# Weight conversion at every second group, four tiles of v ahead of u, and the order of one attention group's work

## The chip, the cores and the metric

The kernel runs on one core of a Trainium2 chip. The metric is the device time of one execution in microseconds (us). The core has TensorE for matmuls (PE in the profile, PEld for its weight loads), VectorE (DVE), ScalarE (ACT), GpSimd (POOL) and SyncE (SP), which issues the DMAs here. Each engine works through its own queue in program order, and semaphores hold an instruction until what it reads is there.

## The reference, cut to what matters

Three blocks follow one another: banded attention, a gated MLP that mixes tokens, and a second mixer. The change touches the first, and the first products of the second.

```python
# attention: 2 batches, 8 heads, 768 positions, 64 per head
keep = is_sink | in_window          # first 4 positions, or the last 128
a = softmax(where(keep, q @ k.T / 8, -1e9))
x = (a @ v) -> [2, 768, 512]
# gated MLP
h = relu(x @ w_in);  u, v = h[..., :512], h[..., 512:]
v_n = layer_norm(v)
gated = u * (w_spatial @ v_n + b_spatial);  x2 = gated @ w_out
# mixer: w_tok1, w_tok2 over tokens, w_ch1, w_ch2 over channels -> out
```

The weights come as 64-bit floats. A float32 product is made of three products of a high and a low half (`mm3`, lines 55 to 60).

## The kernel before, in words

**Attention** is 24 groups `g`: 12 blocks `j` of 128 rows (6 for each batch), each in two phases of four heads (`ph` 0 and 1). `banded` (lines 339 to 399) is a software pipeline, written out by hand: iteration `n` holds a piece of several groups. In the order of the program these are the reciprocal row sums of group n+1 (`sums`, line 195, DVE), the transposes of the weights of group n (`a_transpose`, line 267, PE) and their copies out of PSUM (`a_out`, ACT line 275 and DVE line 278, tiles aT and aL), the scaling of group n+1 (`norm`, lines 246 to 250, POOL and ACT), the scores of group n+3 (`qk` on PE, line 188, `scores` on DVE, lines 213 to 218), the exponentials of group n+2 (`expo`, ACT, line 234); then `v_step` (POOL, line 285) and `sink_parts` (ACT and POOL, lines 257 to 259) on even n, `split_vs` at n = 1 and 13 (ACT line 156, DVE line 158), `step` (the next piece of a pending layer norm, lines 547 to 551), `pump` at n = -1 to 6 and a last `flush` at n = 7; then weights times values of group n-1 (`pv`, line 301, PE), and on even n the sink products (`sinks_mm`, line 320) and `x_out` (ACT line 329, DVE line 330), which writes the high and the low half of x^T (tiles xTH, xTL); last `sinks` on odd n, and `fill`.

**The conversion of w_in** is what `pump` does: one chunk of 128 rows by 512 columns takes three bit operations on DVE (lines 481, 485, 488); its high half is copied by ACT (line 499) and its low half subtracted by POOL (line 500) in the `flush` that the next `pump` calls. Four chunks belong to v (`w_v`) and four to u (`w_u`). `prefetch` keeps two chunks' loads ahead on SP's queue (line 462).

**The filler**: `fill` (line 433) gives PE products of x with w_in, up to a budget of 1900 per iteration, as soon as the needed block of x is there (`xdone`, one iteration after `x_out`). A v tile is four steps of cost 680 and ends in a Relu on ACT and a layer norm; a u tile is four steps of cost 520 and ends in a Relu. `start_x` (lines 418 to 424) lists them: for each batch and half three v tiles, then four u tiles. `fill_until` (line 441) forces a tile before `x_out` overwrites the block that it reads. What is left goes to `mlp` (lines 671 to 674) ahead of the gate products.

**PSUM**: the v and u tiles and the transposed sink weights share two buffers (tag fl); weights times values have one (tag pv), free again after both halves of `x_out`; the transposes have one (tag tr), free after aT and aL.

Of the kernel before, what the change touches and what calls it, by code (L numbers as in the profile page):

```python
# [8 lines left out]
F32R = mybir.dt.float32r  # L9
I32 = mybir.dt.int32  # L10
U32 = mybir.dt.uint32
AF = mybir.ActivationFunctionType
ALU = mybir.AluOpType
PSUM = bass.MemoryType.PSUM

P = 128
B, H, S, D = 2, 8, 768, 64
NB = S // P
DM = H * D
# [5 lines left out]
SK = 8  # L25
SR = 3 * 4 * SK
# [3 lines left out]
NG = B * NB * 2  # L30

LQ, LE, LN = 3, 2, 1
PUMPS = range(-1, 7)
BUDGET = 1900


def f32(ap):
    return ap.bitcast(F32)


class Kernel:
# [106 lines left out]
            nc.sync.dma_start(out=raw[0:SR], in_=self.vs[b])  # L148
            self.vsraw = raw

    def split_vs(self, b):

        nc = self.nc
        raw = self.vsraw
        t = self.vsb[b] = self.ap.tile([P, DM], F32R, name="vs", tag="vs", bufs=1)
        nc.scalar.activation(out=t[0:SR], in_=raw[0:SR], func=AF.Copy)
        r = slice(4 * SK, 8 * SK)
        nc.vector.tensor_tensor(out=t[r], in0=raw[r], in1=f32(t[r]), op=ALU.subtract)

    def slots(self, j):  # L160

# [177 lines left out]
    def banded(self):  # L339
        self.q, self.vb, self.vsb, self.ps_s, self.ss, self.e, self.sm, self.rs = {}, {}, {}, {}, {}, {}, {}, {}  # L340
        self.aT, self.ps_x, self.aS, self.dv, self.eS = {}, {}, {}, {}, {}
        NJ = B * NB
        self.kr = self.ap.tile([P, NC4, RING, KW], F32, name="kr")
        self.vf = self.ap, "vf", 2
        self.scalar_loads(self.cp)
        self.load_qk(0, 2)
        self.warm(10)
        self.load_qk(1)
        self.prefetch()
        self.load_v(0)  # L350
        self.load_qk(2)
        self.masks(self.ap)
        for n in range(-LQ, NG + 2):
            j, ph = divmod(n, 2)
            self.xdone = self.xnext
            if ph and n >= -1:
                if (n + 7) // 2 < NJ:
                    self.load_qk((n + 7) // 2)
                if (n + 3) // 2 < NJ:
                    self.load_v((n + 3) // 2)  # L360
            if 0 <= n + LN < NG:
                self.sums(n + LN)
            if 0 <= n < NG:
                self.a_transpose(n)
                self.a_out(n)
            if 0 <= n + LN < NG:
                self.norm(n + LN)
            if n + LQ < NG:
                self.qk(n + LQ)
                if n < 0:  # L370
                    self.warm(3)
                self.scores(n + LQ)
            if 0 <= n + LE < NG:
                self.expo(n + LE)
            if 0 <= n < NG and ph == 0 and j % NB:
                self.v_step(j)
                self.sink_parts(j)
            if n in (1, 13):
                self.split_vs(n // 12)
            self.step()  # L380
            if n in PUMPS:
                self.pump()
            if n == max(PUMPS) + 1:
                self.flush()
            if 0 <= n - 1 < NG:
                self.pv(n - 1)
                if ph == 0:
                    if (j - 1) % NB:
                        self.sinks_mm(j - 1)

                    self.fill_until(j - 1)
                    self.x_out(j - 1)
            if 0 <= n < NG and ph == 1 and j % NB:
                self.sinks(j)
            if n == NG - 4:
                self.raws = [self.spatial_load(r) for r in range(2)]
            self.fill(BUDGET)
        self.xdone = self.xnext
        self.vf = self.sp, "tmp", 4


    def start_x(self):

        self.xT = self.pair(("XH", "XL"), [P, NC4, S], "xT")
        self.w_v = self.pair(("WA", "WB"), [P, NC4, 512], "wv")
        self.w_u = self.pair(("UC", "UD"), [P, NC4, 512], "wu")
        self.wq, self.wstarted, self.wdone, self.half = [], 0, 0, None
        for c in range(NC4):
            self.queue_weight(self.w_in, slice(c * P, c * P + P), (512, 1024), tuple(x[:, c] for x in self.w_v))
        for c in range(NC4):  # L410
            self.queue_weight(self.w_in, slice(c * P, c * P + P), (0, 512), tuple(x[:, c] for x in self.w_u))
        self.vn = [self.pair((f"{x}H", f"{x}L"), [P, NB, 512], "vn") for x in "VN"]
        self.uT = [self.unit(f"U{b}", [P, NC4, S], F32, "uT") for b in range(B)]
        self.xdone = self.xnext = -1
        self.raws = []
        self.later = []

        self.fills = []
        for b in range(B):
            for half in range(2):  # L420
                for t in range(3 * half, 3 * half + 3):
                    self.fills.append((b * NB + t, b * NB + t, self.v_tile(b, t)))
                for d in range(NC4):
                    self.fills.append((b * NB + 3 * half + 2, b * NB + 3 * half, self.u_tile(b, d, half)))
# [238 lines left out]
    def mlp(self):  # L663
# [57 lines left out]
        slabs = [self.pair(x, [P, 4, DM], "c2") for x in (("WA", "WB"),)]  # L721
        self.w_ch2 = {}

        def queue_ch2(f):
            self.w_ch2[f] = tuple(x[:, f % 4] for x in slabs[f // 4])
            self.queue_weight(self.w_c2, slice(f * P, f * P + P), (0, DM), self.w_ch2[f])

        slabs = [self.pair(x, [P, 4, DM], "c2") for x in (("WA", "WB"),)]
        self.w_ch2 = {}

        def queue_ch2(f):
            self.w_ch2[f] = tuple(x[:, f % 4] for x in slabs[f // 4])
            self.queue_weight(self.w_c2, slice(f * P, f * P + P), (0, DM), self.w_ch2[f])

        slabs = [self.pair(x, [P, 4, DM], "c2") for x in (("WA", "WB"),)]
        self.w_ch2 = {}

        def queue_ch2(*fs):
            for f in fs:
                self.w_ch2[f] = tuple(x[:, f % 4] for x in slabs[f // 4])  # L740
# [1 line left out]

        queue_ch1(0, (2, 3))
        queue_ch2(0, 1, 2)
        queue_ch1(1, (2, 3))
        queue_ch2(3)
        for b in range(B):
            for j in range(2):
                self.tok1_tile(b, j)
                pump()  # L750
        slabs += [self.pair(x, [P, 4, DM], "c2") for x in (("UC", "UD"), ("VH", "VL"))]
        queue_ch2(4, 5)
        queue_ch1(2, (2, 3))
        queue_ch2(*range(6, NF))
# [13 lines left out]
        for n in range(NCH * NF + 1):  # L768
            if n < NCH * NF:
                ch, f = divmod(n, NF)  # L770
# [172 lines left out]
```

## Time and profile before

| what | value |
|---|---|
| median of 3 runs | 496.29 us (495.05 to 496.36) |
| the profiled execution | 494.53 us |
| its span, first to last instruction | 492.7 us |
| mean granted TensorE clock | 0.984 |
| busy: PE, DVE, ACT, POOL | 468.9, 279.7, 178.8, 146.7 us |
| attention and the filler | from the start to about 164 us |

A row of the timeline reads: start in us, duration in us, engine, line, operation, the tile written and the tiles read, and shapes; in brackets the idle time of the engine just before and what ended it. A row of the windows reads: the stretch, its length, then for each engine busy us and, in parentheses, its instructions; then the granted TensorE clock as a share of full speed, the DMA engines' share, and GB/s.

### The profile page before, as it was taken

How to read it: one execution, taken by the hardware profiler on the slowest of the kernel's cores; microseconds unless marked ns; L12 is line 12 of the kernel's file. 1: busy time of each engine (PE TensorE's matmuls, PEld its weight loads, DVE VectorE, ACT ScalarE, POOL GpSimd, SP SyncE). 2: the span in 40 equal slices, each digit the busy share in tenths (PEclk: the TensorE clock that was granted, in tenths of full speed). 3: DMA queues.
4: the chain of work that ended last, by engine and by line, in shares of the span. 5: the costliest groups of instructions: out<-in, count | busy, mean ns of one | idle time of the engine just before them, and what ended most of it. 6: DMA issues, size and time to landing. Idle time of an engine off the chain costs nothing.

```text
span 492.7 us, 6952 instructions
## 1 busy us (share of the span) xinstructions
PE 468.9 (95%) x2562; PEld 391.6 (79%) x2562; DVE 279.7 (57%) x633; ACT 178.8 (36%) x483; POOL 146.7 (30%) x164
## 2 busy tenths in 40 slices
PE   8579899999999999999999899999999999999994
PEld 7357687788898999988888578888888888888883
DVE  6899855866546399837989797666312211311112
ACT  4566876887655222335532222221002100010000
POOL 1356751363544566733443132223000000000000
PEclk9879899999999999999999999999999999999999
DMA  8745142202023032305544144220010000200002
GB/s 260 244 151 175 46 143 68 67 23 87 0 85 130 1 108 69 103 0 151 151 147 130 43 137 122 90 95 26 34 53 1 0 1 0 86 1 0 1 0 92
DMA packets 19722, 38.48 MB, mean 78 GB/s; under 512 B 1824, under 2 KB 8224, under 8 KB 19680
## 3 DMA queue, kind: packets, MB, share of 16 engines
q1 hardware_dynamic: 19248, 37.69, 24.1%
q8 instruction: 22, 0.36, 0.3%
q10 hardware_dynamic: 432, 0.26, 0.2%
q14 instruction: 20, 0.16, 0.1%
HBM read 34.80 MB, written 3.15 MB: 77 GB/s over the span
## 4 chain that ended last, share of the span: by engine, by line
PE 77%; DVE 14%; ACT 5%; issue 2%; POOL 1%; POOLq 0%; ACTq 0%
PE pso L60 7%; PE pso L58 7%; PE pso L59 7%; PE psc L60 6%; PE psc L58 6%; PE psc L59 6%; PE psg L58 3%; PE psg L60 3%; PE psg L59 3%; PE pv L301 3%; DVE wi L485 2%; PE ps L60 2%; PE ps L59 2%; PE ps L58 2%; ACT e L234 2%; PE psu L58 2%
## 5 line engine op out<-in xcount | busy, mean ns | idle before, releaser
L647 DVE SCALAR_TENSOR_TENSOR hh<-psc,hh 128x512 fp32r<-128x512 f32 x36 | 24.9, 691 | 128.0 <-ACT hh L646 127.9
L646 ACT ACTIVATE hh<-psc 128x512 fp32r<-128x512 f32 x36 | 21.5, 597 | 157.2 <-PE psc L60 157.2
L60 PE MATMUL pso<-c2H,hh 128*128 128x512 f32 x144 | 56.3, 391 | 1.1 <-DVE hh L647 1.1
L58 PE MATMUL pso<-c2H,hh 128*128 128x512 f32 x144 | 56.9, 395 | 0.0
L59 PE MATMUL pso<-c2L,hh 128*128 128x512 f32 x144 | 56.0, 389 | 0.0
L488 DVE SCALAR_TENSOR_TENSOR wi<-rawi,wi 128x512 int32<-128x512 int32 (+2 forms) x46 | 40.3, 876 | 1.6
L234 ACT ACTIVATE e<-s,nm 128x136 f32<-128x136 f32 (+1 forms) x96 | 37.6, 393 | 3.9 <-DVE nm L218 3.9
L485 DVE SCALAR_TENSOR_TENSOR wi<-rawi,wi 128x512 int32<-128x512 int32 (+2 forms) x46 | 36.4, 790 | 1.6
L481 DVE TENSOR_SCALAR wi<-rawi 128x512 int32<-128x512 int32 (+2 forms) x46 | 32.5, 707 | 1.4 <-POOL c1L L500 1.2
L60 PEld LDWEIGHTS pso<-c2H,hh 128*128 128x128 f32 x144 | 27.0, 188 | 7.3 <-DVE hh L647 1.6
L59 PE MATMUL psg<-wsTL,vnH 128*128 128x384 f32 x96 | 32.1, 334 | 0.0
L58 PE MATMUL psg<-wsTH,vnH 128*128 128x384 f32 x96 | 32.1, 334 | 0.0
L60 PE MATMUL psg<-wsTH,vnL 128*128 128x384 f32 x96 | 32.1, 334 | 0.0
L59 PEld LDWEIGHTS pso<-c2L,hh 128*128 128x128 f32 x144 | 27.1, 188 | 5.5
L58 PEld LDWEIGHTS pso<-c2H,hh 128*128 128x128 f32 x144 | 27.0, 188 | 5.3
L188 PE MATMUL sc<-kr,q 64*128 64x264 f32 (+2 forms) x192 | 28.7, 417 | 0.4 <-DVE nm L218 0.2
L60 PE MATMUL psc<-u2H,c 128*128 128x512 f32 x72 | 28.0, 389 | 0.0
L58 PE MATMUL psc<-u2H,c1H 128*128 128x512 f32 x72 | 28.0, 389 | 0.0
L60 PE MATMUL psc<-u2H,c1L 128*128 128x512 f32 x72 | 28.0, 389 | 0.0
L58 PE MATMUL psc<-u2H,c 128*128 128x512 f32 x72 | 28.0, 389 | 0.0
L59 PE MATMUL psc<-u2L,c 128*128 128x512 f32 x72 | 28.0, 389 | 0.0
L59 PE MATMUL psc<-u2L,c1H 128*128 128x512 f32 x72 | 28.0, 389 | 0.0
(143 smaller groups left out, 1106.6 us busy)
## 6 DMA issues: line engine op xcount, KB each, us to landing
rawi<-in_moe_w_ch SPq DMA_DIRECT2D x24, 512.0 KB, 3.5
rawi<-in_moe_w_in SPq DMA_DIRECT2D x8, 512.0 KB, 5.0
v<-in_v SPq DMA_DIRECT2D x12, 256.0 KB, 3.7
out_x<-o SPq DMA_DIRECT2D x12, 256.0 KB, 2.4
kr<-in_k SPq DMA_DIRECT2D x11, 272.0 KB, 4.7
q<-in_q SPq DMA_DIRECT2D x11, 256.0 KB, 4.6
raws<-in_w_spT SPq DMA_DIRECT2D x6, 384.0 KB, 4.1
rawi<-in_moe_w_out SPq DMA_DIRECT2D x4, 512.0 KB, 5.7
```

Of the source, the lines that this page charges most:

```text
L58: self.nc.tensor.matmul(ps, lh, rh, start=(first and i == 0), stop=False)
L59: self.nc.tensor.matmul(ps, lh, rl, start=False, stop=False)
L60: self.nc.tensor.matmul(ps, ll, rh, start=False, stop=(last and i == n - 1))
L188: nc.tensor.matmul(o, q[r, p, :], k, start=True, stop=True)
L234: nc.scalar.activation(out=self.e[j][:, 4 * ph + c, :u], in_=s[:, c, :u], func=AF.Exp, bias=nm[:, c : c + 1], scale=-1.0, accum_out=sm[:, ...
L301: nc.tensor.matmul(ps[h * D : (h + 1) * D, p, :], w[:, (2 * p + h) * D : (2 * p + h + 1) * D], self.aT[g][c][:, 2 * x + h, :], start=(p == ...
L481: V.tensor_scalar(out=wi, in0=hi, scalar1=3, scalar2=0x3FFFFFFF, op0=ALU.logical_shift_left, op1=ALU.bitwise_and,)
L485: V.scalar_tensor_tensor(out=wi, in0=hi, scalar=-0x40000000, in1=wi, op0=ALU.bitwise_and, op1=ALU.bitwise_or)
L488: V.scalar_tensor_tensor(out=wi, in0=lo, scalar=29, in1=wi, op0=ALU.logical_shift_right, op1=ALU.bitwise_or)
L646: nc.scalar.activation(out=h, in_=ps, func=AF.Relu)
L647: nc.vector.scalar_tensor_tensor(out=l, in0=ps, scalar=0.0, in1=f32(h), op0=ALU.max, op1=ALU.subtract)
```

## The change

The pumps run at n = -1, 0, 1, 2, 3, 5, 7, 9, and the last flush at n = 10. `split_vs` is cut in two: ACT's part at n = 2 and 14, DVE's part at n = 3 and 15. `pv`, `sinks_mm`, `fill_until` and `x_out` stand ahead of `v_step`, `sink_parts`, `split_vs`, `step` and the pump. The filler's list has four v tiles, four u tiles, two v tiles, four u tiles for each batch. In `mlp` two repeated definitions of the same slabs and of `queue_ch2` are gone; a third one, which stood after them, stays.

```diff
-PUMPS = range(-1, 7)
+PUMPS = (-1, 0, 1, 2, 3, 5, 7, 9)
@@ split_vs
-    def split_vs(self, b):
+    def split_vs(self, b, part):
-        t = self.vsb[b] = self.ap.tile([P, DM], F32R, name="vs", tag="vs", bufs=1)
-        nc.scalar.activation(out=t[0:SR], in_=raw[0:SR], func=AF.Copy)
-        r = slice(4 * SK, 8 * SK)
-        nc.vector.tensor_tensor(out=t[r], in0=raw[r], in1=f32(t[r]), op=ALU.subtract)
+        if part == 0:
+            t = self.vsb[b] = self.ap.tile([P, DM], F32R, name="vs", tag="vs", bufs=1)
+            nc.scalar.activation(out=t[0:SR], in_=raw[0:SR], func=AF.Copy)
+        else:
+            t = self.vsb[b]
+            r = slice(4 * SK, 8 * SK)
+            nc.vector.tensor_tensor(out=t[r], in0=raw[r], in1=f32(t[r]), op=ALU.subtract)
@@ banded
                 self.expo(n + LE)
+            if 0 <= n - 1 < NG:
+                self.pv(n - 1)
+                if ph == 0:
+                    if (j - 1) % NB:
+                        self.sinks_mm(j - 1)
+
+                    self.fill_until(j - 1)
+                    self.x_out(j - 1)
             if 0 <= n < NG and ph == 0 and j % NB:
                 self.v_step(j)
                 self.sink_parts(j)
-            if n in (1, 13):
-                self.split_vs(n // 12)
+            if n in (2, 3, 14, 15):
+                self.split_vs(n // 12, n % 2)
             self.step()
             if n in PUMPS:
                 self.pump()
             if n == max(PUMPS) + 1:
                 self.flush()
-            if 0 <= n - 1 < NG:
-                self.pv(n - 1)
-                if ph == 0:
-                    if (j - 1) % NB:
-                        self.sinks_mm(j - 1)
-
-                    self.fill_until(j - 1)
-                    self.x_out(j - 1)
@@ start_x
-                for t in range(3 * half, 3 * half + 3):
+                for t in range((0, 4)[half], (4, 6)[half]):
```

## Rows read from the trace of the kernel before

**Rows 1.** Busy time in stretches of the span (columns as told above)

```profile
28.00:33.30 5.30, 4.25 (x27) 2.89 (x24) 5.13 (x16) 3.64 (x14) 3.38 (x4) 0.50 0.87 282
...
54.00:57.50 3.50, 3.50 (x17) 2.59 (x14) 3.40 (x13) 2.15 (x10) 2.42 (x4) 0.51 0.01 2
...
66.00:72.00 6.00, 5.43 (x48) 4.62 (x48) 2.80 (x18) 4.00 (x18) 1.88 (x2) 1.00 0.08 25
90.00:142.00 52.00, 51.84 (x413) 42.58 (x413) 34.31 (x126) 37.40 (x125) 25.61 (x42) 1.00 0.14 42
142.00:164.00 22.00, 21.82 (x115) 20.06 (x114) 10.95 (x13) 10.00 (x17) 11.85 (x12) 1.00 0.34 120
```

**Rows 2.** PE's waits for x^T's low half, whole run: total us, times, the longest

```profile
PE pv L301 <- DVE xTL L330: 3.4, 4, 1.6
```

**Rows 3.** Timeline of DVE, iterations n = 0 to 2, and its wait at n = 8

```profile
17.48 1.23 DVE L195 TENSOR_SCALAR r<-sums 128x4 f32<-128x4 f32 x1
...
21.84 0.68 DVE L158 TENSOR_TENSOR vs<-vsraw,vs 32x512 fp32r<-32x512 f32 x1 [1.13 <-ACT vs L156]
22.55 1.42 DVE L481 TENSOR_SCALAR wi<-rawi 128x512 int32<-128x512 int32 x1
...
25.34 0.16 DVE L195 TENSOR_SCALAR r<-sums 128x4 f32<-128x4 f32 x1
...
28.01 0.42 DVE L481 TENSOR_SCALAR wi<-rawi 128x512 int32<-128x512 int32 x1
...
29.81 0.68 DVE L330 TENSOR_TENSOR xTL<-pv,xTH 128x512 fp32r<-128x512 f32 x1
...
62.77 0.69 DVE L330 TENSOR_TENSOR xTL<-pv,xTH 128x512 fp32r<-128x512 f32 x1 [0.81 <-ACT xTH L329]
```

**Rows 4.** Timeline of POOL and ACT: two low halves, and one high half of a chunk

```profile
16.94 1.74 POOL L500 TENSOR_TENSOR wvL<-wi,wvH 128x512 fp32r<-128x512 f32 x1 [2.20 <-ACT wvH L499]
22.40 1.29 POOL L500 TENSOR_TENSOR wvL<-wi,wvH 128x512 fp32r<-128x512 f32 x1 [2.77 <-ACT wvH L499]
57.53 0.61 ACT L499 ACTIVATE wuH<-wi 128x512 fp32r<-128x512 f32 x1
```

**Rows 5.** Timeline of PE, iterations n = 3, 5 and 7

```profile
26.44 0.87 PE L267 MATMUL tr<-ident,e 128*128 128x128 f32 x4 [2.86 <-DVE aL L278]
...
30.55 0.69 PE L301 MATMUL pv<-aT,v 128*64 128x128 f32 x4 [1.05 <-DVE xTL L330]
...
41.55 0.44 PE L301 MATMUL pv<-aT,v 128*64 128x128 f32 x4 [0.65 <-DVE xTL L330]
...
53.29 0.44 PE L301 MATMUL pv<-aT,v 128*64 128x128 f32 x4 [1.59 <-DVE xTL L330]
...
55.35 0.63 PE L59 MATMUL psv<-wvL,xTH 128*128 128x512 f32 x1
55.78 0.63 PE L60 MATMUL psv<-wvH,xTL 128*128 128x512 f32 x1
...
57.74 0.39 PE L59 MATMUL psv<-wvL,xTH 128*128 128x512 f32 x1
57.96 0.40 PE L60 MATMUL psv<-wvH,xTL 128*128 128x512 f32 x1
```

**Rows 6.** Timeline of PE, iterations n = 8 to 11: transposes and products of u

```profile
58.20 0.60 PE L267 MATMUL tr<-ident,e 128*128 128x128 f32 x4
...
62.09 0.34 PE L58 MATMUL psu<-xTH,wuH 128*128 128x384 f32 x1
...
63.67 0.60 PE L267 MATMUL tr<-ident,e 128*128 128x128 f32 x4
...
67.38 0.44 PE L58 MATMUL psu<-xTH,wuH 128*128 128x384 f32 x1 [0.57 <-ACT aS L313]
...
77.16 0.33 PE L60 MATMUL psu<-xTH,wuL 128*128 128x384 f32 x1
77.57 0.44 PE L58 MATMUL psu<-xTH,wuH 128*128 128x384 f32 x1
```

More of the change, by code (lines that the diff above doesn't have):

```diff
@@ L374, in banded @@
                 self.expo(n + LE)
-            if 0 <= n < NG and ph == 0 and j % NB:
-                self.v_step(j)
-                self.sink_parts(j)
-            if n in (1, 13):
-                self.split_vs(n // 12)
[L380 to L384, printed above, removed]
             if 0 <= n - 1 < NG:
@@ L392, in banded @@
                     self.x_out(j - 1)
+            if 0 <= n < NG and ph == 0 and j % NB:
+                self.v_step(j)
+                self.sink_parts(j)
+            if n in (2, 3, 14, 15):
+                self.split_vs(n // 12, n % 2)
+            self.step()
+            if n in PUMPS:
+                self.pump()
+            if n == max(PUMPS) + 1:
+                self.flush()
             if 0 <= n < NG and ph == 1 and j % NB:
@@ L722, in mlp @@
         self.w_ch2 = {}
[L724 to L736, printed above, removed]
         def queue_ch2(*fs):
```

## The prediction

> **What bounds the kernel now.** I read the waits of TensorE first, then the busy time by stretches, then the timelines of PE, DVE, ACT and POOL around the largest waits. From 90 us to the gate products near 164 us PE is busy 51.84 of 52 us and 21.82 of 22 [rows 1]: there PE is the bound. The waits stand earlier, between 20 and 68 us, and what ends most of them is DVE: a transpose waited 2.86 us for aL, and weights times values waited 1.05, 0.65 and 1.59 us for the low half of x^T [rows 5], nearly all of the 3.4 us that PE spends in that wait [rows 2]. DVE was late because conversion sits ahead of what PE needs: a chunk's three bit operations take 1.80 us (28.01 to 29.81) and stand ahead of `x_out`, and `split_vs` made DVE idle 1.13 us and then work 0.68 [rows 3]. After two of these waits PE ran at a granted clock of 0.50 and 0.51 [rows 1], its 1.2 GHz level: products of v follow at 0.43 us (55.35 to 55.78) in place of 0.22 (57.74 to 57.96) [rows 5].
>
> So I count PE's time. Up to the gate its work is the same before and after, only in another order; its end moves by the change of its idle time plus that of its half-speed time.
>
> **The change part by part**, against the profiled execution: its time of 494.53 us is a span of 492.7 and 1.83 around it, and it lies 1.76 below the median of the runs, 496.29. I subtract the sum from the median.
>
> 1. *split_vs in two.* DVE was free at 20.71 (21.84 less 1.13) and began the conversion at 22.55 [rows 3]; now it begins at 20.71 and all behind it comes 1.84 us sooner, the aL that ends the 2.86 us wait too: -1.85. DVE's half (0.68) goes to n = 3, where it finds ACT's half done. The conversion's first operation took 1.42 us here against 0.42 at n = 2, beside a subtraction of 1.29 us on POOL (22.40), and the row sums took 1.23 us beside the one at 16.94 [rows 3, 4]: DVE stood still until POOL was through. At 28.01 nothing stood still. By the rows alone both are possible, so this term lies between -1.85 (the same hold) and -2.85 (none), and I take the first, since POOL's subtraction is still issued there. The Trainium skill (SBUF — State Buffer, section "Who interferes with whom") says that DVE and GpSimd share a port pair as an exclusive lock, and that whoever starts first makes the other wait; by it the hold stays at n = 1, POOL starting amid the three operations, and the sum is mine; without it the sum would be 1.0 lower.
>
> 2. *Values and `x_out` first; no conversion at n = 4 and 6.* The low half of x^T no longer has 1.80 us of conversion ahead of it. The three waits go: -(1.05 + 0.65 + 1.59) = -3.3 [rows 5]. What is late next is ACT's high half, behind the exponentials; DVE already waits 0.81 us for it at 62.77 [rows 3], and at n = 2 this wait now stands ahead of a conversion. It is on DVE, in the time that the removed conversion leaves free. Behind the waiting `x_out` stand, on DVE, layer norm's pieces and the pump, and on ACT sink parts, the high halves and the Relu of v; none of these is needed by PE within its next few products, except in term 6.
>
> 3. *The half-speed stretch of 54.0 to 57.5 us.* It followed the 1.59 us wait, and PE was the bound in it. Seven products 0.21 us slower each [rows 5]: -1.4 if it does not come back, 0 if it does. The one of 28.0 to 33.3 I leave at nothing: DVE was busy 5.13 of those 5.30 us [rows 1] and set the pace.
>
> 4. *The last chunk of v.* It is still flushed at n = 3, while PE comes 2 to 3 us sooner to the first v tile's last products. Between nothing and one whole subtraction of 1.29 us [rows 4]; POOL comes sooner too, so +0.3.
>
> 5. *No filler at n = 8.* Only the third v tile's last step is left there. Three steps of u, 62.09 to 63.67 [rows 6], move behind the fourth v tile. The work is not lost, but if DVE and ACT are not ready for the next transpose, PE idles: between 0 and +1.6. DVE has 1.80 us of conversion more at n = 7, so I take +1.4.
>
> 6. *The crowd at n = 10.* The last flush, a layer norm and the fourth v tile's Relu now fall into one iteration, and the second u tile of n = 11 needs the buffer that the sink copy frees after the exponentials. Its counterpart at n = 9 waited 0.57 us [rows 6]. New in that chain are the flush's high half, 0.61 on ACT [rows 4], and one hold of the row sums, 1.23 less the 0.16 at 25.34, 1.07 us [rows 3]: +1.7. The lower bound is 0; the upper is 1.7 and the 1.4 by which PE comes sooner without the slow stretch, 3.1.
>
> 7. *u tiles out of step with the iterations.* At n = 17 and 19, and once ahead of the gate, a u tile now begins behind the sinks as at 77.57, which came 0.41 us after the product before it in place of 0.17 [rows 6]: three times 0.24, +0.7; bounds 0 and three times 0.57.
>
> The rest at nothing. The conversions at n = 7 and 9: DVE is busy 2.80 of the 6 us from 66 to 72 [rows 1]; without that cover 1.80 each. SP's loads of u's chunks: two iterations lie between the uses. `fill_until` now forces two steps at n = 14 and two at n = 20: PE does them anyway and is the bound. The second batch's split: also there. The repeated definitions issue no instruction.
>
> Sum: -1.85 - 3.3 - 1.4 + 0.3 + 1.4 + 1.7 + 0.7 = -2.45. Predicted: 496.29 less 2.4, 493.9 us. A measurement tells some 0.3% (1.5 us) from no change.
>
> **The rivals.**
>
> *A, all of it is given back (496.4 us).* Terms 4 to 6 at their upper bounds (1.3 + 1.6 + 3.1) with term 7 at 0.7 make +6.7 against -6.55. For it: PE is the only bound from 90 us on, so every product of u that is put off is paid later in full. Against: the chain of term 6 is not full everywhere, the wait at 67.38 was only 0.57.
>
> *B, slower by 2.3 (498.6 us).* The wait of n = 11 brings a half-speed stretch back where PE is the bound. The two stretches of [rows 1] follow waits of 2.86 and 1.59 us; after the 0.57 of 67.38 the clock stayed at 1.00. So it decides somewhere between 0.57 and 1.59, and 0.57 + 1.7 lies above. Its price is half of 3.5 to 5.3 us, 1.75 to 2.65, with nothing to hide it, 2.2 taken, and it comes on top of A's 0.15. Against: the waits at 26 and 53 us stood among several others, this one stands alone amid dense work. The Trainium skill (TensorE: Matmul & The Clock Gate, section "HAM oscillation — how this bites in real kernels") speaks against the change here: idle gaps throw the array back to half rate and each gap is paid again in slow products; the rows at 28 and 54 us agree.
>
> *C, the gain comes whole (490.8 us).* Terms 4, 6 and 7 at 0, term 5 at 1.0: -5.5. For it: ACT is busy 4.00 of 6 us from 66 to 72 [rows 1], so the flush may fit. Against: it takes POOL and DVE out of each other's way at every iteration.
>
> That the move does nothing is a part of A: PE's own order is the same, and where PE is late, DVE waits for it at `x_out`.
>
> **How the numbers follow.** Forecast 0.45 (its own range -1.0 to -3.9), A 0.25, B 0.17, C 0.13. Faster by over 0.3%: three quarters of the forecast (0.34) and all of C, 0.47. Slower: B but for 0.04, and 0.04 from A's upper half, 0.17. The rest, 0.36, is no change. The range runs from near C to near B, 491.0 to 498.0.
>
> **What would show it.** Right: no conversion between a group's scores and `x_out`, the pv waits for x^T near 0, the 2.86 us wait near 1.0, no stretch at 0.5 after 40 us, the transposes of n = 8 to 10 some 5 us or more sooner with fewer products done, and a wait of about 2.3 us for the sink copy at n = 11. The gate's first product, at 164 us before, should come 2.4 us sooner. Wrong: a low clock between 60 and 80 us (B), or waits for the flush in the first v tile above 1.3 us; and any change of the time behind the gate, where I expect none.

## The result, and the profile after

The changed kernel took 501.15 us in the median of 7 runs (498.27 to 502.1); the kernel before took 495.86 us beside it (7 runs, 493.99 to 496.36). The ratio is 1.0107, with a 95% interval of 1.0091 to 1.0124: slower by 5.3 us, above the predicted range. The profiled execution has a span of 500.2 us and a mean granted clock of 0.975. A profile shows one execution only: that of before took 494.53 us, 1.3 less than the median beside it, and that of the changed kernel 502.1, the longest of its seven, so differences between two profiles of under some 2 us say little by themselves (of three kernels with the same code up to there, before, e3_list and e7_list_b0 below, the transpose of n = 7 came at 49.19, 49.76 and 51.07 us).

The first thing to read is again busy time by stretches, now of the changed kernel (stretch, length, busy us and instructions of PE, PEld, DVE, ACT, POOL, then the granted clock, the DMA share and GB/s):

```profile
28.00:33.30 5.30, 5.30 (x32) 4.26 (x31) 5.13 (x16) 3.09 (x13) 2.32 (x2) 0.69 0.28 105
54.00:57.50 3.50, 3.50 (x34) 2.54 (x32) 3.43 (x12) 2.68 (x11) 1.71 (x2) 1.00 0.02 7
62.00:65.30 3.30, 2.75 (x19) 2.36 (x20) 2.78 (x13) 2.48 (x8) 3.03 (x6) 0.51 0.04 12
66.00:72.00 6.00, 6.00 (x50) 5.09 (x49) 4.48 (x14) 4.62 (x19) 3.73 (x3) 1.00 0.34 106
79.00:82.40 3.40, 3.40 (x14) 2.80 (x14) 0.00 (x0) 0.91 (x3) 0.39 (x1) 0.52 0.00 0
90.00:142.00 52.00, 51.76 (x398) 41.50 (x398) 31.20 (x116) 36.04 (x123) 21.37 (x35) 1.00 0.12 42
142.00:164.00 22.00, 19.92 (x113) 17.78 (x114) 10.99 (x18) 10.70 (x18) 10.39 (x11) 1.00 0.34 120
280.00:283.40 3.40, 3.40 (x13) 2.71 (x14) 0.97 (x2) 0.60 (x1) 0.00 (x0) 0.57 0.06 22
```

Against [rows 1]: the half-speed stretch at 54 us is gone (0.51 before, 1.00 now), but there are three others, at 62, 79 and 280 us. And from 142 to 164 us PE is busy 19.92 us in place of 21.82: the bound that I counted on just ahead of the gate is no longer one. PE's waits say for what (total us, times, the longest):

```profile
PE tr L270 <- DVE aL L281: 3.4, 4, 1.4
...
PE psu L58 <- ACT aS L316: 2.3, 1, 2.3
...
PE pv L304 <- DVE xTL L333: 1.4, 3, 0.6
PE psv L58 <- ACT uT L566: 1.3, 1, 1.3
...
PE psu L58 <- ACT uT L566: 0.8, 1, 0.8
```

The same waits before the change:

```profile
PE tr L267 <- DVE aL L278: 3.0, 2, 2.9
...
PE psu L58 <- ACT aS L313: 0.6, 1, 0.6
...
PE psu L58 <- ACT uT L563: 0.2, 1, 0.2
```

The wait for x^T's low half fell from 3.4 us [rows 2] to 1.4. The waits for aL stayed near 3 us in all, but there are four of them now in place of two. Two others grew: the one for the sink copy aS from 0.6 to 2.3, those for the Relu of u (uT) from 0.2 to 2.1.

To see where the time goes I used the transposes as a ruler: one starts per iteration. That of n = 3 came at 25.09 us against 26.44 [rows 5], that of n = 8 at 54.84 against 58.20 [rows 6], 3.36 us sooner. Then the lead goes: the one of n = 10 came at 67.26 us against 69.07, with three steps of u (1.58 us [rows 6]) still to be done, that of n = 13 at 86.68 against 85.06. The last, n = 23, where equally many products have been done in both, came at 137.91 against 133.69; the 2.6 us between n = 13 and 23 are mostly products that the list had put off (e3_list below, which has the new list alone, gives back 2.62 there). The gate's first product came at 170.31 against 163.93, 6.4 us later. So three losses are to be found: between n = 8 and 10, at n = 11, and between the last transpose and the gate. From the gate on the changed kernel needed another 1.1 us (329.9 against 328.8), with the clock of 0.57 at 280 us.

The first loss, in the timeline of all engines from n = 7 to n = 9 (start, duration, engine, line):

```profile
55.79 0.42 DVE L484 TENSOR_SCALAR wi<-rawi 128x512 int32<-128x512 int32 x1
...
56.01 1.35 POOL L503 TENSOR_TENSOR wuL<-wi,wuH 128x512 fp32r<-128x512 f32 x1 [1.66 <-ACT wuH L502]
...
56.25 1.66 DVE L488 SCALAR_TENSOR_TENSOR wi<-rawi,wi 128x512 int32<-128x512 int32 x1
...
57.95 0.69 DVE L491 SCALAR_TENSOR_TENSOR wi<-rawi,wi 128x512 int32<-128x512 int32 x1
58.55 0.16 DVE L198 TENSOR_SCALAR r<-sums 128x4 f32<-128x4 f32 x1
...
59.02 0.71 ACT L253 ACTIVATE e<-e,r 128x136 f32<-128x136 f32 x2 [2.35 <-DVE r L199]
...
59.65 0.68 PE L270 MATMUL tr<-ident,e 128*128 128x128 f32 x4 [0.77 <-DVE aL L281]
...
61.45 0.49 PE L191 MATMUL sc<-kr,q 64*128 64x128 f32 x4 [0.46 <-DVE nm L221]
...
62.55 0.69 PE L304 MATMUL pv<-aT,v 128*64 128x128 f32 x4 [0.61 <-DVE xTL L333]
63.03 0.64 PE L304 MATMUL pv<-aL,dv 128*64 128x128 f32 x4
```

The conversion at n = 7 holds DVE from 55.79 to 58.55 us, with 1.66 us for an operation of 0.69 while POOL subtracts the chunk of n = 5. Behind it stands the reciprocal r that ACT waits 2.35 us for, and aL. PE, which has only one step of products at n = 8, waits 0.77, 0.46 and 0.61 us and then multiplies at half speed: 0.64 us where the same products take 0.39.

The last loss, ahead of the gate:

```profile
150.74 1.56 ACT L580 ACTIVATE wsTH<-raws 128x768 fp32r<-128x768 f32 x2
...
151.97 1.76 SPq L573 DMA_DIRECT2D raws<-in_w_spT  x4
...
155.12 0.84 ACT L580 ACTIVATE wsTH<-raws 128x768 fp32r<-128x768 f32 x1 [2.44 <-issue]
155.87 0.85 ACT L566 ACTIVATE uT<-psu 128x384 f32<-128x384 f32 x2
...
156.39 0.50 PE L58 MATMUL psv<-wvH,xTH 128*128 128x512 f32 x1 [1.31 <-ACT uT L566]
```

ACT stands 2.44 us in front of the next row of w_spatial. The view names no releaser, but the row's load was issued from 151.97 us on, and the loads of these rows took 3.0 us or more to land, which fits a wait for the load. Behind that copy stand the Relus of two u tiles, and until they have run the fifth v tile has no accumulator. Before the change ACT waited for PE here, and not PE for ACT; the last Relu of u was through before the copy of the row:

```profile
147.13 0.49 ACT L563 ACTIVATE uT<-psu 128x384 f32<-128x384 f32 x1 [1.59 <-PE psu L60]
147.51 0.84 ACT L577 ACTIVATE wsTH<-raws 128x768 fp32r<-128x768 f32 x1
```

### The profile page after: what moved, and what is told of

The parts are those of the page before. It is cut to its first block, busy times and chain, and to the rows that moved or that the text cites. A ratio compares the mean times of both kernels' runs of the same rounds, so it can differ in the third digit from the quotient of the medians.

```text
span 500.2 us, 6950 instructions
## 1 busy us (share of the span) xinstructions
PE 473.6 (95%) x2562; PEld 394.3 (79%) x2562; DVE 281.7 (56%) x633; ACT 178.7 (36%) x483; POOL 145.3 (29%) x164
## 4 chain that ended last, share of the span: by engine, by line
PE 77%; DVE 13%; ACT 6%; issue 2%; POOL 1%; ACTq 0%; POOLq 0%
PE pso L60 7%; PE pso L59 7%; PE pso L58 7%; PE psc L60 6%; PE psc L59 6%; PE psc L58 6%; PE psg L59 3%; PE psg L60 3%; PE psg L58 3%; DVE wi L488 3%; ACT e L237 2%; PE ps L59 2%; PE ps L58 2%; PE ps L60 2%; PE sc L191 2%
## 5 line engine op out<-in xcount | busy, mean ns | idle before, releaser
L488 DVE SCALAR_TENSOR_TENSOR wi<-rawi,wi 128x512 int32<-128x512 int32 (+2 forms) x46 | 39.3, 854 | 1.6
L491 DVE SCALAR_TENSOR_TENSOR wi<-rawi,wi 128x512 int32<-128x512 int32 (+2 forms) x46 | 39.2, 852 | 1.6
L484 DVE TENSOR_SCALAR wi<-rawi 128x512 int32<-128x512 int32 (+2 forms) x46 | 31.3, 681 | 2.0 <-DMA rawi<-in_moe_w_ch 2.0
L191 PE MATMUL sc<-kr,q 64*128 64x264 f32 (+2 forms) x192 | 29.9, 427 | 1.4 <-DVE nm L221 0.9
```

The costliest lines, as they stand in the source:

```text
L191: nc.tensor.matmul(o, q[r, p, :], k, start=True, stop=True)
L484: V.tensor_scalar(out=wi, in0=hi, scalar1=3, scalar2=0x3FFFFFFF, op0=ALU.logical_shift_left, op1=ALU.bitwise_and,)
L488: V.scalar_tensor_tensor(out=wi, in0=hi, scalar=-0x40000000, in1=wi, op0=ALU.bitwise_and, op1=ALU.bitwise_or)
L491: V.scalar_tensor_tensor(out=wi, in0=lo, scalar=29, in1=wi, op0=ALU.logical_shift_right, op1=ALU.bitwise_or)
```

## The experiments

Three theories stood at the beginning: late conversions and list of tiles lose, the split and the order gain (1); the order loses (2); the list alone loses (3). The first four kernels do one part each on the kernel before. Ratios are against the kernel before, run beside each on the same chip; a difference in us, here and below, is the ratio less 1 times 495.86 us where nothing else is said.

**e1_split**: `split_vs` in two, at n = 2, 3, 14, 15, and nothing else.

```diff
-            if n in (1, 13):
-                self.split_vs(n // 12)
+            if n in (2, 3, 14, 15):
+                self.split_vs(n // 12, n % 2)
```

> The kernel before with split_vs alone cut in two (ACT's part at n = 2 and 14, DVE's at n = 3 and 15). Theory 1 (the loss comes from the late conversions together with the tile list; split and order only gained): the transpose of n = 3 comes 1.8 us sooner, as it does in the changed kernel, and 1 to 1.9 us of it reach the gate products: 494 to 495 where the kernel before has 495.9, ratio 0.996 to 0.998. Theory 2 (the order of the iteration carries the loss) and theory 3 (the list alone carries it): the same here. Wrong for all: slower than before by over 0.3%.

Measured: 494.02 us, ratio 0.9957 (0.9942 to 0.9973), faster by 2.1 us. In its profile the transpose of n = 3 comes 1.82 us sooner against the one ahead of it, as in the changed kernel (1.83). In that profile the lead does not reach the gate, where 1 to 1.9 us of it were expected: the transpose of n = 4 comes at 35.26 us against 35.29, with PE at half speed until 34.5 us in place of 33.5, and the gate's first product at 164.36 against 163.93. The execution profiled took 496.1 us, the longest of its seven; that the gain in the runs is this lead is not shown.

**e2_order**: pv, sinks_mm, fill_until and both halves of `x_out` ahead of `v_step`.

```diff
+            if 0 <= n - 1 < NG:
+                self.pv(n - 1)
...
+                    self.x_out(j - 1)
             if 0 <= n < NG and ph == 0 and j % NB:
                 self.v_step(j)
```

> The kernel before with pv, sinks_mm, fill_until and x_out moved ahead of v_step, sink_parts, split_vs, step and the pump, all else as before. Theory 1: PE's waits for the low half of x^T fall from 3.4 to under 1.5 us, DVE waits some 0.5 us ahead of the conversions of n = 2, 4 and 6 instead, and the time stays within 1.5 us of before (ratio 0.997 to 1.003). Theory 2: 4 to 6 us slower (1.008 to 1.012), with new waits behind the ninth iteration. Theory 3: as theory 1.

Measured: 497.89 us, ratio 1.0045 (1.0028 to 1.0063), slower by 2.2 us. PE's waits in its profile:

```profile
PE tr L267 <- DVE aL L278: 7.5, 5, 3.0
...
PE pv L301 <- DVE xTL L330: 0.8, 2, 0.4
```

The wait for xTL is nearly gone, as forecast, and 4.5 us of waits for aL have come (7.5 us against 3.0; in e3_list, e4_pumps_list, e7_list_b0 and e8_pumps_early, which keep the old order, 3.3 to 4.4). DVE's and PE's timeline at n = 4 and 5 shows the exchange:

```profile
40.82 0.69 DVE L330 TENSOR_TENSOR xTL<-pv,xTH 128x512 fp32r<-128x512 f32 x1 [0.51 <-ACT xTH L329]
41.43 0.42 DVE L481 TENSOR_SCALAR wi<-rawi 128x512 int32<-128x512 int32 x1
41.88 1.66 DVE L485 SCALAR_TENSOR_TENSOR wi<-rawi,wi 128x512 int32<-128x512 int32 x1
43.58 0.69 DVE L488 SCALAR_TENSOR_TENSOR wi<-rawi,wi 128x512 int32<-128x512 int32 x1
...
45.27 0.66 DVE L278 TENSOR_TENSOR aL<-tr,lowT 128x512 f32<-128x512 f32 x1
...
46.08 0.46 PE L267 MATMUL tr<-ident,e 128*128 128x128 f32 x2 [0.98 <-DVE aL L278]
```

DVE idles 0.51 us for ACT's copy with the conversion ready behind it, and then does the conversion between xTL and aL.

**e3_list**: four tiles of v ahead of u's first, in both sequences.

```diff
-                for t in range(3 * half, 3 * half + 3):
+                for t in range((0, 4)[half], (4, 6)[half]):
```

> The kernel before with the filler's list alone changed: four v tiles, four u, two v, four u for each batch; pumps at n = -1 to 6. Theory 1: the missing filler of n = 8 costs PE up to 1.6 us, the waits ahead of the gate (1.3 and 0.8 us for the Relu of u in the changed kernel) come too, but the crowd at n = 10 lacks the flush and the wait for the sink copy at n = 11 stays under 1.3 us without a half-speed stretch behind it: 2 to 4 us slower, ratio 1.004 to 1.008. Theory 2: within 1.5 us of before. Theory 3: the whole loss and the gain of the other parts on top, 6 us or more, 1.012 and up.

Measured: 497.83 us, ratio 1.0048 (1.003 to 1.0066), slower by 2.4 us. Its profile loses 0.5 us up to the last transpose and 1.9 from there to the gate, with the wait of psv for uT, 1.4 us.

**e4_pumps_list**: that list and the late conversions together (the conversions need it: with three tiles of v a product of u would come ahead of its weights).

```diff
-PUMPS = range(-1, 7)
+PUMPS = (-1, 0, 1, 2, 3, 5, 7, 9)
```

> The kernel before with the list and the pumps of the changed kernel (n = -1, 0, 1, 2, 3, 5, 7, 9, flush at 10), but split_vs whole at n = 1 and the order of the iteration as before. Theory 1: the whole loss and without the gain of the split: 5 to 8 us slower than before, ratio 1.010 to 1.016, with the wait of 2 us or more for the sink copy at n = 11 and a half-speed stretch behind it. Theory 2: within 2 us of before. Theory 3: as the list alone, within 1.5 us of it.

Measured: 500.88 us, ratio 1.0095 (1.0079 to 1.0111), slower by 4.7 us, 2.3 above e3_list by the ratios and 3.1 by the medians. That is just below the 5 to 8 us of theory 1, and its mechanism did not come: the wait for the sink copy was 1.23 us, not 2, with the clock at 1.00 behind it. So theory 1 was right on the list, near on split and conversions, and wrong on the order and on how the conversions cost; theories 2 and 3 each name a part. The next four ask for the mechanisms.

**e5_half_ahead**: the order with DVE's half of `x_out` left in its old place.

```diff
-                    self.x_out(j - 1)
+                    self.x_high(j - 1)
...
+            if 0 <= n - 1 < NG and ph == 0:
+                self.x_low(j - 1)
```

> Only the order moves, and of x_out only half of it: pv, sinks_mm, fill_until and ACT's copy to x^T's high half go to where the change puts them, DVE's subtract for the low half stays behind step and the conversions as before. e2_order, where both halves moved, took +2.2 us (ratio 1.0045) and PE's waits for aL rose to 7.5 us in its profile. Theory 4 (the loss is DVE's subtract: it waits at the head of DVE's queue for ACT's copy, and the conversions and the next aL stand behind it): the loss goes, 494.5 to 496.3, PE's waits for aL below 5 us, and since the high half is early the waits of pv for xTL (4.5 us in the run with the split alone) fall too. Theory 5 (the loss is on ACT: sink values, layer norm's vnH and the weights' high halves come behind the copy): the loss stays, 497.3 to 498.3.

Measured: 494.29 us, ratio 0.9962 (0.9949 to 0.9975). Theory 4 holds: with DVE's half behind, the loss of 2.2 us is gone, and the waits for aL are back at 3.0 us. DVE at n = 4 now converts while ACT copies, and aL starts at 43.16 us, not 45.27:

```profile
39.68 0.42 DVE L486 TENSOR_SCALAR wi<-rawi 128x512 int32<-128x512 int32 x1
...
41.48 0.68 DVE L333 TENSOR_TENSOR xTL<-pv,xTH 128x512 fp32r<-128x512 f32 x1
...
43.16 0.66 DVE L278 TENSOR_TENSOR aL<-tr,lowT 128x512 f32<-128x512 f32 x1
```

The waits for xTL did not fall, though (3.5 us against 3.4), and its profile has the same span as that of before, 492.7 us, which lies 1.3 us under its median: where the gain of 1.9 us by the ratio lies, the profiles don't show.

**e6_split_half**: e1_split and e5_half_ahead together.

> The split in two parts (alone 2.1 us faster, ratio 0.9957) together with ACT's half alone ahead. Theory 4: the sum of e1_split and e5_half_ahead or better, 492.5 to 494.2, which is the fastest so far. Theory 5: 495.2 to 496.2, the split's gain given back by ACT's queue.

Measured: 492.33 us, ratio 0.9928 (0.9915 to 0.9942), faster by 3.6 us, the lowest median of all (e10_split_half_b0 below can't be told from it); it beats both kernels.

**e7_list_b0**: four tiles of v ahead in the first sequence alone.

```diff
-                for t in range(3 * half, 3 * half + 3):
+                k = 4 - b
+                for t in range((0, k)[half], (k, 6)[half]):
```

> The list with four tiles of v ahead of u for the first sequence of the batch alone; the second keeps three. e3_list, with four in both, took +2.4 us; its profile put +0.5 us before the last transpose and +1.9 us between it and the first product of the gate, where PE waits 1.4 us in the products of the second sequence's last v tiles for a Relu of u that stands behind the copy of a row of w_spatial. Theory 6 (the loss lies in the second sequence's list, just ahead of the gate): 495.7 to 496.6, no wait of psv for uT over 0.5 us. Theory 7 (it lies in the first sequence, where u's tiles come later): 497.2 to 498.2 still.

Measured: 494.74 us, ratio 0.9991 (0.9976 to 1.0006), no change that can be told, and a little under theory 6's range. The loss of e3_list was the second sequence's list, just ahead of the gate. All the profiles agree on the place: from the last transpose to the gate's first product it is 32.15 to 32.40 us in the four kernels with the second list (the changed one, e3, e4, e8) and 30.24 to 30.26 in the ten without it. ACT's wait ahead of the copy (2.44 to 2.67 us) stands in these four alone. ACT there, with no Relu left behind a late copy:

```profile
149.40 0.49 ACT L564 ACTIVATE uT<-psu 128x384 f32<-128x384 f32 x1 [1.58 <-PE psu L60]
149.78 0.84 ACT L578 ACTIVATE wsTH<-raws 128x768 fp32r<-128x768 f32 x1
```

**e8_pumps_early**: e4_pumps_list with the last two conversions at 6 and 7, so that the last flush leaves n = 10.

```diff
-PUMPS = (-1, 0, 1, 2, 3, 5, 7, 9)
+PUMPS = (-1, 0, 1, 2, 3, 5, 6, 7)
```

> As e4_pumps_list (list of four in both sequences and conversions at -1, 0, 1, 2, 3, 5, 7, 9: 500.9 us, +4.7), with the last two conversions at 6 and 7 in place of 7 and 9, so that the last flush comes at n=8 and not at n=10. Theory 8 (the conversions themselves are harmless late, it is the last flush among layer norm, the first Relus of u and the sinks of n=10 to 12 that costs): about 498.0, e3_list's time and a little, 497.6 to 498.6, and the step of 3.0 us at n=10 goes. Theory 9 (the loss is that any conversion behind n=6 leaves the products of u without their weights or DVE without room): 499.5 to 501.

Measured: 501.02 us, ratio 1.0099 (1.0085 to 1.0113), as slow as e4_pumps_list. My theory 8, that the flush among layer norm and sinks was the whole loss, fell, and theory 9's time (499.5 to 501) came. What the two kernels share is the conversion at n = 7, and ACT stands behind it in this one:

```profile
60.64 0.71 ACT L250 ACTIVATE e<-e,r 128x136 f32<-128x136 f32 x2 [2.33 <-DVE r L196]
```

**e10_split_half_b0, e11_last_at_7, e9_after_mended, e12_after_list_b0** build the change up from e6_split_half, one thing at a time: e10 adds the first sequence's list; e11 moves the last conversion from n = 6 to 7, and with it the last flush from n = 7 to 8; e9 has the change's conversions (-1, 0, 1, 2, 3, 5, 7, 9); e12 puts DVE's half of `x_out` ahead as well; only the second list is then missing to the changed kernel. The edit of e11 on e10:

```diff
-PUMPS = range(-1, 7)
+PUMPS = (-1, 0, 1, 2, 3, 4, 5, 7)
```

> The changed kernel with two of its parts mended: DVE's half of x_out goes back behind step and the conversions (ACT's half stays ahead), and the list of four tiles of v holds for the first sequence alone. The late conversions stay. If the parts add up (the split -2.1, order with ACT's half alone -1.6, list in the first sequence -0.9, late conversions on such a list +3.1 us, from the medians of e1, e6 less e1, e7, and e4 less e3): 494.0 to 495.2. If the late conversions only cost together with DVE's held subtract or with the second list: 491.0 to 492.8.

> The same with the conversions as before, at -1 to 6. What separates it from e9_after_mended is the price of the late conversions in the changed kernel's surroundings. Adding up: 492.33 less 0.9, so 490.8 to 492.4, the fastest of all, and e9_after_mended 2.5 to 3.5 us above it. If the gain of the list in the first sequence was that of the half-speed stretch at 54 us, which the split takes away as well: no better than e6_split_half, 492.0 to 493.0.

> As e10_split_half_b0, with one conversion moved by one iteration: the last at n=7 in place of 6 (n=6 has none). Theory 10 (the loss of the late conversions is the one at n=7: in e4_pumps_list and e8_pumps_early it holds DVE from 56.6 to 59.9 us, ahead of the reciprocal that ACT's weights wait for 2.3 us and of aL at n=8, just where PE has no products left): 1.5 to 3.0 us above e10. Theory 11 (it is the sum of small shifts, the gaps at 4 and 6 and the late end): at most 0.6 us above e10.

> The changed kernel with one part mended: four tiles of v ahead of u in the first sequence alone, the second keeps three; order and late conversions as in the change. It lies between e9_after_mended (497.3 us, where DVE's half of x_out is mended too) and the changed kernel (501.15 us), and says which of the two mended parts those 3.85 us were. Theory 12 (with the conversions at -1, 0, 1, 2, 3, 5, 7 and 9 only the one at n=2 still stands behind DVE's subtract, which runs in even iterations, so the order costs little here, and the second list is the loss): 497.3 to 498.6. Theory 13 (the order costs here what it costs alone, 3.6 us between e2 and e5): 499.5 to 501.

Measured:

| kernel | median us | ratio (interval) | us against before | step |
|---|---|---|---|---|
| e1_split | 494.02 | 0.9957 (0.9942 to 0.9973) | -2.1 | -2.1 split |
| e10_split_half_b0 | 493.03 | 0.9945 (0.9925 to 0.9964) | -2.7 | -0.6 ACT's half ahead, first list |
| e11_last_at_7 | 495.98 | 1.0005 (0.9989 to 1.0022) | +0.2 | +3.0 last conversion at 7, not 6 |
| e9_after_mended | 497.3 | 1.0038 (1.0024 to 1.0052) | +1.9 | +1.6 conversions at 7 and 9 |
| e12_after_list_b0 | 497.7 | 1.0051 (1.003 to 1.0072) | +2.5 | +0.6 DVE's half ahead |
| the change | 501.15 | 1.0107 (1.0091 to 1.0124) | +5.3 | +2.8 second list |

The interval of a step is some 1.1 to 1.3 us either way (the two ratios' own, added as squares). So three steps are shown: the conversion at n = 7, the second list (2.8 here and 2.8 by e3_list less e7_list_b0; 1.9 to 2.2 in the profiles), and the split; that of the conversion at 9 is just outside its error, and the other two are not told from nothing. Theory 10 (the conversion at n = 7) and theory 12 (the order costs little in the change) hold. The order's 2.2 us alone and its 0.6 here go together: with the change's conversions only the one of n = 2 still falls into an even iteration, where `x_out` is. In the profiles of these two the exchange is there even so: from e9 to e12 the waits for xTL fall from 3.0 to 1.2 us, and those for aL rise from 2.9 to 4.6.

My sum for e9_after_mended missed by 2 us: the late conversions cost 4.6 us there, more than in e4 less e3; why more is open. e10 took the time of its second case, with the first list worth nothing beside the split. That case's reason is not shown: it was that the split takes away the half-speed stretch at 54 us, and in e10's own profile this stretch stands (0.60 from 54.0 to 57.5 us).

What the conversion at n = 7 does is seen in the stretch behind it, in e11 and, second fence, e10:

```profile
62.00:65.30 3.30, 2.73 (x19) 2.36 (x20) 2.26 (x6) 1.94 (x4) 3.20 (x5) 0.59 0.15 46
78.00:82.00 4.00, 4.00 (x39) 3.22 (x38) 1.83 (x10) 3.31 (x13) 0.00 (x0) 1.00 0.17 43
```

```profile
62.00:65.30 3.30, 3.30 (x34) 2.69 (x33) 2.77 (x13) 2.48 (x8) 3.02 (x6) 1.00 0.88 245
```

In the 3.3 us from 62 us, PE issues 19 products in place of 34. The transposes give the size. From n = 8 to n = 10 PE has the same products in these kernels; they took 8.42 us in e10, and 12.68 in e11 and 12.66 in e9, with the half-speed stretch. They took 11.11 in e12, whose waits are the same (0.78, 0.46 and 0.61 us) but whose clock stayed at 1.00:

```profile
62.00:65.30 3.30, 3.08 (x26) 2.61 (x27) 2.78 (x15) 2.48 (x10) 2.83 (x5) 1.00 0.00 0
```

So, as an estimate from these four profiles, the waits make some 2.7 us of it and the clock some 1.6; the gain ahead of n = 8, since n = 6 has no conversion any more, comes off. All twelve runs of e11 (494.57 to 497.61 us) lie above all seven of e10 (492.01 to 494.32).

The conversion at n = 9 and the flush at n = 10 show one stretch later, where e11 is at full speed. e9's stretch and the wait ahead of it:

```profile
78.00:82.00 4.00, 4.00 (x19) 2.86 (x17) 0.56 (x2) 1.79 (x7) 0.57 (x1) 0.61 0.00 0
```

```profile
PE psu L58 <- ACT aS L316: 2.0, 1, 2.0
```

In e11 this wait is 0.3 us.

## Why the prediction was wrong

The sign was wrong. By the forecast's own terms:

**Term 1 (split, -1.85): right in size,** -1.83 us at n = 3 in the profile and -2.1 us in the runs, though e1_split's profile does not show the one becoming the other. The conversion began at 21.11 us, 1.44 us sooner; its first operation was not held (0.42 us), but the row sums behind it were, 1.25 us:

```profile
21.11 0.42 DVE L484 TENSOR_SCALAR wi<-rawi 128x512 int32<-128x512 int32 x1
...
22.37 1.76 POOL L503 TENSOR_TENSOR wvL<-wi,wvH 128x512 fp32r<-128x512 f32 x1 [2.25 <-ACT wvH L502]
...
22.91 1.25 DVE L198 TENSOR_SCALAR r<-sums 128x4 f32<-128x4 f32 x1
```

The hold by POOL went to another instruction, and cost the same. The rule cited there from the Trainium skill (SBUF — State Buffer, section "Who interferes with whom"), that the one who starts first makes the other wait, agrees with these rows.

**Term 2 (values and `x_out` first, -3.3): failed.** The named waits did fall, from 3.4 to 1.4 us, and to 0.8 in e2_order. But the step said of DVE's wait for ACT that it lies "in the time that the removed conversion leaves free", and of what stands behind it that none is needed by PE soon. The row sums' reciprocal and aL stand behind it, and the next transposes wait for them: 4.5 us more in e2_order. In the change, too, the waits for xTL went over into waits for aL (e9 and e12), and the order was worth little either way (steps of -0.6 with the first list, and +0.6). So the -3.3 did not come; this is the largest miss of the sum, 3.3 of the 7.7 us between forecast and result.

**Terms 3 (half-speed stretch gone, -1.4) and rival B.** The stretch at 54 us went; others came at 62 and 79 us, the second in B's place and the first in one that nobody named. But the stretch at 54 us did not hang on the wait alone. The wait of 1.58 or 1.59 us at n = 7 stands in eight profiles; behind it the clock fell to 0.50 in four (before, e5, e7, e10) and stayed at 1.00 in four (e1, e3, e6, e8), in e3 with the same code up to there as before:

```profile
53.87 0.44 PE L301 MATMUL pv<-aT,v 128*64 128x128 f32 x4 [1.58 <-DVE xTL L330]
```

```profile
54.00:57.50 3.50, 3.50 (x30) 2.89 (x30) 3.40 (x11) 1.59 (x8) 3.02 (x5) 1.00 0.01 2
```

So the -1.4 was a price taken from one execution, and the median of before need not hold it. B's wait for the sink copy came, 2.3 us, and the stretch behind it too. Its point of decision lay, said B, between 0.57 and 1.59 us; the wait of 1.27 us in e1_split (at 67.66 us) and that of 1.23 in e4_pumps_list (78.64) had no stretch behind them, the clock being 1.00 for 8 us after, while that of 2.0 in e9_after_mended had one, and so had one of 1.27 for xTL in e4_pumps_list (64.00). With n = 7 as above, the length of a wait alone does not decide it in these traces. B's price of 2.2 us does not come on top of term 6: the whole step is 1.6.

**Term 5 (no filler at n = 8, +1.4; bounds 0 and 1.6): mis-sized.** The mechanism was named, with the conversion of n = 7 in it, but bounded by PE's three missing steps. What is lost is DVE's chain and, where it comes, the half-speed stretch behind it: 3.0 us for this one conversion. The conversion itself was taken at 1.80 us and lasted 2.76 (55.79 to 58.55), since POOL holds the middle one, and "the conversions at n = 7 and 9" stood among the things at nothing, covered by DVE's slack from 66 to 72 us: the wrong stretch, as the conversion of n = 7 is over at 58.55.

**Term 6 (crowd at n = 10, +1.7): right in size,** 1.6 us (e9 less e11, an interval of 1.1 either way), with the wait for the sink copy that was forecast.

**Term 7 (u tiles out of step, +0.7; bounds 0 and 1.7): failed, the largest miss among the losses.** The u tile "ahead of the gate" was priced by a delay behind the sinks. It is a Relu on ACT behind a copy that waits for a load, and the v tile behind it waits for its accumulator: 2.8 us by the runs, 1.9 to 2.2 in the profiles. [Rows 1] had PE busy 21.82 of 22 us there, and I took this for a property of the stretch; it was one of the order of tiles in it.

**Term 4 (+0.3)** shows nothing: PE has no wait for the low half of v's last chunk.

So of -6.55 us of gains only the split and at most 0.6 came, and of +4.1 us of losses nearly the double, 7.4 to 8.0.

**Open:** the time behind the gate, where I expected no change. The stretch at 280 us in the changed kernel stands in seven of the fourteen profiles, somewhere between 272 and 284 us: in e1, e3, e4, e8, e9, e11 and the changed kernel, and not in before, e2, e5, e6, e7, e10 and e12. In e1_split, which differs from before only far ahead of it:

```profile
272.00:278.00 6.00, 4.05 (x15) 3.43 (x16) 3.01 (x6) 0.75 (x2) 1.29 (x1) 0.72 0.31 87
```

Whether it comes follows from no single edit that I made. From the gate's first product to the end it is 329.4 to 329.9 us with it and 328.0 to 329.1 without, so it makes one profile some 1 us better or worse than another. Where e5's gain lies, which its profile doesn't show, was not settled.

## What to carry to other kernels

An operation that waits for another engine should not be put ahead of ready work on an in-order queue: splitting a two-engine step so that the producer's half goes early and the consumer's half stays behind the ready work took away a loss of 2.2 us, and with the split of `split_vs` it makes the kernel with the lowest median here, e6_split_half. Before work is moved to a later iteration, look at what the engine does in exactly that iteration and at what PE has to do meanwhile: 1.8 us of DVE work cost 3.0 us one iteration later, where PE's filler had just been taken away (a late conversion with the filler left in place was not tried). A stretch in which an engine is fully busy proves nothing for another order of work in it; go through the queues of the engines that free its buffers, with their loads. And before a stretch of one profile is priced, see whether other executions have it: two of the stretches here came in some profiles and not in others with the same waits ahead of them.

## What the runs showed of the hardware

A half-speed stretch needs no single long wait: in the changed kernel 0.77, 0.46 and 0.61 us within 4 us were followed by a clock of 0.51, while a single one of 1.27 us amid dense products (e1_split) was not. Nor do the same waits bring it each time: 0.78, 0.46 and 0.61 us in e12 were followed by 1.00, and the 1.59 us at n = 7 by 0.50 in some profiles and 1.00 in others.

What POOL's subtractions hold up on DVE depends on the operation. In the traces of before and after, the conversion's operations and the row sums (all from SBUF) lasted up to 1.67 us and 1.26 us beside one, in place of 0.69 and 0.17. The low half of x^T, read from PSUM, took 0.68 to 0.69 us in all 12 cases of before, 6 of which began while a subtraction ran, and layer norm's statistics 0.68 to 0.70. So in these traces the step that reads an accumulator lay beside POOL's work at no cost, while the conversion was held up at times.
